# Regrouping a fused attention and adapter kernel: gate groups, DMA turns, squares, x copies and stores

## The chip, the cores and the metric

The kernel runs on one core of a Trainium2 chip. The metric is the device time of one execution in microseconds. A core has a matrix engine (PE, with weight loads shown as PEld), a vector engine (DVE), a scalar engine (ACT), a general engine (POOL) and a sync engine (SP). Each works through its own instructions in order. They wait for each other on semaphores. Transfers are issued from SP, ACT and POOL and run on 16 DMA engines.

## The reference

Two stages follow each other. The first is attention with a squared relu instead of a softmax; its result, with the heads side by side, is x. The second adds to each row of x the outputs of its two best of eight low-rank adapters.

```python
batch, n_heads, seq, head_dim = (8, 12, 448, 64)
scores = scale * np.matmul(q, k.transpose(0, 1, 3, 2))
attn = np.maximum(scores, 0.0) ** 2 / S
x = np.matmul(attn, v)                   # then (8 * 448, 768)
logits = x @ w_gate                      # 8 experts, the best 2 kept
w = softmax over the two kept logits
delta[rows of e] += w * ((x @ A[e]) @ B[e])   # A: 768 x 16, B: 16 x 768
return x + delta
```

## The kernel before, in words

**Tiling.** A batch has 448 rows. Its 12 heads are worked in three sets of four heads (a quad, q), two of them on each half of the 128 partitions. The 448 keys are cut into seven blocks of 64 (j). One step n is one batch, one quad and one key block. The last batch is cut once more, into its first 320 queries (one key block a step) and its last 128 (four key blocks a step). That makes 174 steps, numbered in the order in which they run: 21 for each batch, 27 for the last. n below 126 is batches 0 to 5, n from 126 batch 6, n from 147 batch 7.

**A step.** POOL issues the loads of q, k and v (L185). `tp` turns q and k on PE through the identity (L310), and DVE copies them out to qT (L324). `qk` makes the scores of four heads, keys on the partitions, in two PSUM banks (L449). `relu` scales them, applies the relu and writes bf16 into a tile of the pool `a`, on ACT (L468) or DVE (L470). `sq` squares a whole tile of `a` on DVE (L485). `pv` multiplies v with it and adds over the seven key blocks in PSUM (L516). After the last block `xt_copy` casts the result into `xt`, which holds x turned, channels on partitions (L544). The pairs of steps that share a tile of `a`, and so a square, follow the cycle 2, 2, 3 (`sqs`), at most 2688 columns (`GROUP`).

**The adapters.** The 3584 rows of x form 28 tiles of 128. A gate group of up to three tiles is worked at once. `z` multiplies x with the gate and all A (L560). On DVE come a top-8 per tile (`gmax`, L581) and the small operations `gd`, `gu`, `gt`, `gw` (L585 to L600); the sigmoid of ACT (`gsg`, L597) gives the two weights; `gzp` scales z (L604). `zt` turns it on PE (L622), and `zT` copies it out (L639). Then each tile is done in two halves of 384 columns. `b` (L705, L714) makes three matmuls with the identity that turn x back, and one product with B in float32 that shows as two MATMULs. `o` (L743) evacuates a half to a tile of the pool `osb` on ACT or DVE. `st` (L760) stores it.

**Turned tiles.** For tiles 15 to 23 (`xback`) the identity matmuls are left out. Instead SP turns x back with six DMA transposes for each three tiles (`xb`, L655), and the evacuation, then on DVE only, adds the turned x (L734). Each turn waits for the x copies of its tiles and, with `xlag=6`, for the store of the tile six before.

**The store.** Rows are permuted inside a batch: 64 consecutive rows of a tile are one j, and land in the output seven rows apart. So `st` issues two transfers of 64 rows for a tile. The last tile is stored as two halves, from SP and ACT. Tiles 24 and 26 are stored from ACT, all others from SP.

**Order.** `build` makes the operations with their dependencies and the pool buffers that they take and give. The string `ORDER` is a list written out ahead of time: every operation by name and number, with its PSUM bank (`@4`) and, where it can run on two engines, its engine (`:A`, `:D`). Each engine gets its operations in that order. Names such as `f64` are loads. A position in this list is told below by the relu it stands behind: "at relu140" means after relu140 and before relu141. `POOLS` gives the number of buffers: 11 for `a`, four for `osb`, three for `xb`.

Of the kernel before, what the change touches and what calls it, by code (L numbers as in the profile page):

```python
# [10 lines left out]
BF16 = mybir.dt.bfloat16  # L11
# [3 lines left out]
J = 7  # L15
CUT = 3
SPIN = 8
PH = 64
QUADS = 3
NB = 8  # L20
# [9 lines left out]
PARTS = {b: ((0, S, 1),) for b in range(NB)}  # L30
PARTS.update({7: ((0, 320, 1), (320, 448, 4))})


C = dict(late=6, xi=(), om=(), merge_x=0, sqs=(2, 2, 3), xback=(15, 23), xblat=1.4, xbdur=1.35, bx=8, xlag=6, xh=2, apart=3, apcap=1, gl=(3, 1), tqlat=2.0)
GROUP = 2688
POOLS = dict(qT=5, a=11, zp=2, zT=3, osb=4, w=3, q=5, k=5, v=8, xb=3)
# [3 lines left out]
f4 f3 f1 f0 f2 f6 f5 f8 f7 f11 f9 f10 f84@0 f12 f88 f85@2 f90 f89 f13 f87@4 qk0@6 f91 qk1@0 qk2@2 relu0:D qk3@4  # L40
f14 relu1:A relu2:D relu3:A tp2@6 f17 qk4@0 relu4:A te2 qk5@4 qk6@2 sq2 relu5:A tp3@6 f16 f86@0 relu6:A te3 sq0
qk7@0 f15 qk8@4 qk9@6 relu7:A tp4@2 relu8:D relu9:A f18 qk10@0 te4 qk11@4 relu10:A qk12@6 sq4 tp5@2 relu11:A f19
qk13@0 relu12:A te5 tp6@4 f26 relu13:A sq9 qk14@2 qk15@6 tp7 relu14:A f23 sq7 pv0@0 pv1 pv2 relu15:A pv3 qk16@2
te6 pv4 pv5 relu16:A f20 pv6 qk17@6 x13:D pv7@4 relu17:A qk18@2 sq11 pv8 f22 pv9 x12:A qk19@6 relu18:A pv10
qk20@0 relu19:D f21 pv11 relu20:A pv12 pv13 qk21@2 x27:A sq16 qk22@6 f27 qk23@0 relu21:A aw1@5 sq14 relu22:A f33
relu23:A x26:D qk24@2 tp8@6 ae1 f25 relu24:A qk25@0 sq18 qk26@4 tp9 relu25:A f55 pv14@2 pv15 pv16 relu26:A pv17
te8 qk27@0 pv18 f31 pv19 relu27:A pv20 sq23 qk28@4 qk29@6 x41:A f28 qk30@0 relu28:A x40:D aw0@3 sq25 relu29:A
f29 relu30:A qk31@4 tp10@6 ae0 tp11 relu31:A f32 sq21 qk32@0 qk33@2 relu32:A te10 pv21@4 pv22 f30 relu33:A pv23
qk34@0 sq30 qk35@6 relu34:A qk36@2 f37 relu35:D relu36:A qk37@0 pv24 pv25 pv26 relu37:A sq32 qk38@2 f35 tp12@6
pv27 relu38:A tp13 qk39@0 x55:A te12 f43 qk40@2 x54:A z0@5 relu39:A sq35 qk41@6 f34 z1 relu40:A qk42@0 relu41:D  # L50
z2 relu42:A qk43@2 f38 gmax0 relu43:A tp14@6 sq28 qk44@0 tp15 relu44:A f42 qk45@2 gd0 gu0 te14 relu45:A qk46@0
gt0 relu46:A f50 sq39 qk47@6 pv28@2 pv29 pv30 gsg0 pv31 relu47:A qk48@0 f24 pv32 pv33 gw0 sq44 pv34 relu48:A f48
qk49@6 x69:A gzp0 tp18@0 relu49:A tp19 sq37 f36 pv35@4 zt0@3 zt1 zt2 x68:A qk50@6 te18 zT0:A pv36 f41 pv37
relu50:A qk51@2 pv38 sq46 pv39 relu51:A pv40 qk52@0 f47 qk53@6 pv41 relu52:A tp16@2 x82:D tp17 relu53:A te16
qk54@0 b2@4 relu54:A sq49 f44 qk55@6 o2:A qk56@2 qk57@0 relu55:A relu56:D b0@4 f49 x83:A relu57:D qk58@6 o0:A
qk59@2 relu58:A z3@5 z4 f39 sq51 relu59:A qk60@0 qk61@6 z5 sq56 relu60:A b4@4 f40 relu61:A gmax3 qk62@2 sq58
b1@0 relu62:A f46 gu3 gd3 o4:A qk63@6 gt3 sq42 qk64@2 gsg3 o1:A b3@1 f65 relu63:A gw3 b5@4 gzp3 relu64:A sq60
f51 zt3@0 zt4 zt5 o3:A pv42@6 pv43 o5:A qk65@2 st2 pv44 zT3:A pv45 sq53 qk66@4 relu65:A pv46 pv47 pv48 tp20@0
relu66:A st4 qk67@2 tp21 x96:D x97:A f53 te20 pv49@4 relu67:A pv50 qk68@6 st0 pv51 pv52 relu68:A pv53 sq63 f66
pv54 pv55 qk69@0 qk70@2 x110:A relu69:D qk71@6 f45 relu70:A b6@4 relu71:A x111:D qk72@0 o6:D tp22@2 relu72:A  # L60
sq65 qk73@6 tp23 pv56@4 pv57 relu73:A f74 qk74@0 te22 pv58 pv59 relu74:A pv60 qk75@6 f79 pv61 sq67 pv62 relu75:A
qk76@2 b8@0 relu76:A x124:D qk77@6 f64 x125:A sq70 tp24@2 relu77:A tp25 qk78@4 z6@1 te24 f59 relu78:A qk79@6 z7
relu79:A o8:D qk80@4 qk81@2 f52 sq72 z8 relu80:A b10@0 relu81:A gmax6 sq77 f54 qk82@6 tp26@4 o10:A tp27 qk83@2
relu82:A gd6 gu6 b7@0 te26 f56 relu83:A qk84@6 gt6 o7:D qk85@4 gsg6 relu84:A qk86@2 gw6 f70 sq74 b9@0 relu85:A
pv63@6 pv64 relu86:A gzp6 pv65 qk87@4 pv66 sq79 pv67 relu87:A pv68 pv69 zt6@1 zt7 x139:A x138:D zt8 qk88@2 o9:A
qk89@4 zT6:D qk90@6 relu88:A st8 relu89:D tp28@0 tp29 relu90:A qk91@2 f80 te28 pv70@4 pv71 relu91:A pv72 pv73
qk92@6 f60 sq84 pv74 pv75 relu92:A pv76 qk93@0 b14@2 x153:D x152:A f58 relu93:A sq81 qk94@6 tp30@4 o14:A tp31
pv77@0 relu94:A pv78 f77 qk95@2 te30 pv79 pv80 relu95:A pv81 qk96@6 pv82 f57 sq91 pv83 relu96:A qk97@4 b11@2
relu97:D x166:A f67 b12@3 x167:A o11:A sq93 qk98@6 o12:A st10 qk99@0 qk100@4 relu98:A relu99:D b13@2 relu100:A
z9@3 st6 sq88 qk101@6 o13:A tp32@0 qk102@4 relu101:A tp33 b15@2 st12 f62 sq86 relu102:A qk103@6 o15:A te32 f61  # L70
qk104@4 relu103:A z10 z11 sq100 relu104:A qk105@0 f69 pv84@6 pv85 pv86 relu105:A gmax9 qk106@4 pv87 sq95 f72
pv88 relu106:A pv89 pv90 qk107@0 x181:A qk108@4 f63 gd9 gu9 x180:A relu107:D b16@2 relu108:A gt9 qk109@6 o16:D
f81 pv91@0 gsg9 pv92 relu109:A gw9 pv93 sq105 qk110@4 pv94 pv95 relu110:A pv96 f78 qk111@6 gzp9 pv97 relu111:A
x195:D zt9@2 zt10 qk112@4 sq98 x194:A zt11 f75 b17@3 relu112:A zT9:D qk113@6 o17:A sq102 pv98@0 qk114@4
relu113:A pv99 st16 tp36@2 pv100 tp37 relu114:A pv101 qk115@6 te36 pv102 pv103 relu115:A st14 pv104 tp34@4 tp35
f83 sq109 qk116@2 x209:A qk117@6 x208:A b20@1 relu116:A f68 te34 b22@0 relu117:A f71 sq114 o20:A qk118@2 qk119@4
qk120@6 relu118:A b21@1 f73 sq112 o22:A b23@2 relu119:A o21:D z12@3 sq107 relu120:A st20 qk121@0 qk122@4
relu121:A z13 relu122:D z14 o23:A qk123@6 pv105@0 gmax12 pv106 relu123:A qk124@4 gd12 pv107 gu12 pv108 gt12
sq116 pv109 relu124:A pv110 pv111 qk125@6 f82 b18@2 gsg12 relu125:A gw12 x223:D x222:A qk126@4 f76 o18:D qk127@6
relu126:A b19@1 gzp12 sq121 relu127:A zt12@0 zt13 zt14 qk128@2 pv112@4 pv113 o19:D relu128:A qk129@6 pv114  # L80
zT12:D pv115 st18 pv116 relu129:A pv117 sq123 pv118 tp38@2 qk130@0 x236:A tp39 qk131@6 st22 relu130:A b24@4 te38
relu131:A tp42@0 sq119 tp43 x237:A qk132@2 b25@6 relu132:A te42 xb90 b28@7 o24:A o25:A sq128 xb93 qk133@2 o28:A
qk134@4 tp40@0 relu133:A sq126 pv119@6 tp41 pv120 relu134:A pv121 xb91 qk135@2 te40 pv122 pv123 relu135:A pv124
pv125 qk136@4 x251:D xb94 qk137@0 x250:A b29@2 sq130 relu136:A b26@3 st24 relu137:A sq135 o29:A qk138@6 qk139@4
o26:A qk140@0 xb92 z15@2 relu138:A relu139:D z16 z17 relu140:A qk141@6 st28 gmax15 pv126@4 pv127 relu141:A gd15
pv128 gu15 qk142@0 gt15 sq133 pv129 pv130 gsg15 pv131 relu142:A xb108 qk143@6 pv132 gw15 b27@3 gzp15 x264:A
x265:D relu143:A zt15@2 xb111 zt16 zt17 sq137 pv133@0 o27:A qk144@4 tp44@6 zT15:A pv134 tp45 relu144:A xb95
qk145@2 pv135 te44 pv136 relu145:A pv137 qk146@4 pv138 pv139 st26 sq140 relu146:A z18@6 b30@7 x279:A sq142 z19
x278:A xb109 qk147@2 qk148@4 qk149@0 o30 relu147:A z20 sq144 b32@7 relu148:A xb112 relu149:A b33@2 gmax18 xb110
qk150@4 o32 qk151@0 relu150:A b31@3 gu18 o33 relu151:A gd18 qk152@4 sq149 st32 b34@7 relu152:A gt18 o31 gsg18  # L90
qk153@0 qk154@4 gw18 o34 relu153:A b35@2 st30 gzp18 relu154:A qk155@0 o35 pv140@6 relu155:A pv141 sq151 qk156@4
xb113 pv142 pv143 relu156:A qk157@2 qk158@0 pv144 pv145 relu157:D relu158:A pv146 tp46@4 tp47 x293:A x292:D
qk159@0 qk160@2 relu159:A zt18@7 te46 zt19 xb126 zt20 z21@6 relu160:A z22 sq156 zT18:A qk161@0 qk162@4 qk163@2
relu161:A xb129 b40@7 sq147 relu162:A z23 sq158 relu163:A qk164@0 xb127 pv147@4 pv148 pv149 relu164:A pv150
qk165@2 o40 pv151 pv152 relu165:A pv153 sq154 qk166@0 xb130 b41@7 relu166:A gmax21 x307:A gu21 qk167@2 gd21
pv154@0 sq163 x306:A pv155 pv156 st34 relu167:A pv157 pv158 qk168@4 gt21 o41 pv159 gsg21 pv160 b36@2 gw21 x320:A
gzp21 xb128 x321:A b38@3 sq161 relu168:A zt21@7 zt22 sq165 zt23 qk169@0 st40 zT21:A pv161@4 pv162 pv163
relu169:A pv164 qk170@6 o38 pv165 pv166 relu170:A o36 pv167 xb131 b37@3 x335:D x334:A sq168 qk171@0 qk172@6
relu171:A qk173@4 z24@2 o37 z25 relu172:A sq170 st36 b46@3 relu173:A b47@0 o46 b39@1 sq172 b44@3 o47 z26 o39
# [831 lines left out]
```

## Time and profile before

| | us |
|---|---|
| median of 3 runs (181.49 to 182.18) | 182.09 |
| the profiled execution | 182.88 |
| its span, first to last instruction | 180.8 |
| mean granted PE clock | 0.988 |

One row of the profile's group list is one kind of instruction: how often it ran, its busy time, the mean duration of one. These touch the change:

| group | count | busy us | mean ns |
|---|---|---|---|
| DVE square, 128 x 1792 (L485) | 45 | 48.2 | 1082 |
| DVE square, 128 x 2688 (L485) | 21 | 32.9 | 1572 |
| ACT relu, 128 x 896 (L468) | 132 | 114.6 | 990 |
| ACT cast of x, 128 x 448 (L544) | 28 | 16.1 | 616 |
| DVE cast of x, 128 x 448 (L544) | 14 | 8.7 | 618 |
| PE product with B, 128 x 384 (L714) | 112 | 47.5 | 515 |
| PE identity matmuls of x (L705) | 114 | 12.7 | 220 |
| ACT output copy, 128 x 384 (L743) | 26 | 13.1 | 523 |
| DVE output copy, 128 x 384 (L743) | 12 | 6.7 | 555 |
| DVE output add with turned x (L734) | 18 | 9.7 | 550 |
| SP issue of a turn (L655), median | 18 | | 1264 |
| SP issue of a store (L760), median | 52 | | 588 |

Instructions of one engine overlap: the next one starts before the last has ended, so the time from start to start, which the timeline gives, is less than a duration. A median turn lands 3.1 us after its issue starts.

### The profile page before, as it was taken

The numbers are of one execution on the slowest core, as the hardware profiler recorded it, in microseconds if no ns is written. First come the engines' busy times: TensorE is split into PE (matmuls) and PEld (weight loads), VectorE is DVE, ScalarE is ACT, GpSimd is POOL, SyncE is SP. The second block draws the span as 40 slices with busy tenths as digits, with TensorE's granted clock in tenths as the row PEclk, the third lists the DMA queues.
The fourth block names the chain that finished last, engine by engine and source line by source line (L and its number), as shares of the span: only waits on it lengthen the run. The fifth ranks groups of instructions, "written<-read, shape, count | busy, mean of one in ns | idle before, by whom it ended". The sixth has DMA issues, their size and how long they took to land.

```text
span 180.8 us, 7744 instructions
## 1 busy us (share of the span) xinstructions
PE 165.2 (91%) x3366; PEld 99.2 (55%) x3366; DVE 163.6 (90%) x254; ACT 156.4 (87%) x240; POOL 89.9 (50%) x155
## 2 busy tenths in 40 slices
PE   7777889788999999999999899999999999999990
PEld 2434466454555565655646475655666557676640
DVE  0799799999989999999999899999999999999740
ACT  3499899999999999999999999999999899992120
POOL 7998998979669377760877487340000000000000
PEclk9997899999999999999999999999999999999999
DMA  5999999999999999996599999997376579467875
GB/s 94 127 175 180 156 142 179 182 184 164 214 142 146 186 237 194 176 178 141 68 143 287 224 181 259 224 170 202 68 126 144 131 175 110 101 149 176 227 215 172
DMA packets 34450, 30.50 MB, mean 169 GB/s; under 512 B 11952, under 2 KB 30896, under 8 KB 34416
## 3 DMA queue, kind: packets, MB, share of 16 engines
q0 software_dynamic: 22000, 17.03, 64.9%
q1 hardware_dynamic: 11792, 11.90, 26.5%
q10 hardware_dynamic: 624, 1.08, 2.2%
q8 instruction: 26, 0.43, 1.0%
q14 instruction: 8, 0.07, 0.1%
HBM read 33.84 MB, written 11.01 MB: 248 GB/s over the span
## 4 chain that ended last, share of the span: by engine, by line
PE 51%; ACT 27%; POOL 7%; DMA 6%; issue 4%; DVE 3%; ACTq 0%; DVEq 0%; POOLq 0%
ACT a L468 24%; PE ps L714 18%; PE ps L449 11%; PE ps L516 10%; DMA q<-in_q_dram 6%; PE ps L560 4%; PE ps L310 3%; PE ps L705 3%; POOL q L185 3%; POOL k L185 3%; PE ps L622 2%; ACT osb L743 2%; DVE a L485 2%; ACT xt L544 1%; POOL k_rest L216 1%
## 5 line engine op out<-in xcount | busy, mean ns | idle before, releaser
L468 ACT ACTIVATE a<-ps 128x896 bf16<-128x896 f32 (+3 forms) x158 | 132.6, 952 | 3.7 <-PE ps L449 3.1
L485 DVE TENSOR_TENSOR a<-a 128x1792 bf16<-128x1792 bf16 (+3 forms) x75 | 89.0, 1200 | 0.0
L449 PE MATMUL ps<-qT 64*64 64x448 bf16 (+2 forms) x756 | 58.1, 342 | 3.9 <-ACT a L468 2.4
L714 PE MATMUL ps<-B,zT 128*128 128x384 f32 x112 | 47.5, 515 | 0.0
L516 PE MATMUL ps<-a,v 64*64 64x448 bf16 (+2 forms) x756 | 45.3, 335 | 1.6 <-DVE a L485 1.3
L449 PEld LDWEIGHTS <-qT 64*64 64x64 bf16 x756 | 25.1, 105 | 31.8 <-issue 23.2
L185 POOL DMA_DIRECT2D k<-in_k_dram x46 | 27.9, 629 | 18.2 <-PE ps L310 7.3
L185 POOL DMA_DIRECT2D v<-in_v_dram x48 | 29.0, 629 | 6.2 <-PE ps L449 1.8
L185 POOL DMA_DIRECT2D q<-in_q_dram x48 | 29.4, 651 | 4.9 <-DMA v<-in_v_dram 2.7
L516 PEld LDWEIGHTS <-v 64*64 64x64 bf16 x756 | 22.7, 108 | 9.0 <-issue 4.1
L324 DVE COPY qT<-ps 128x1792 bf16<-128x1792 bf16 x21 | 22.8, 1085 | 0.2
L544 ACT CAST xt<-ps 128x448 bf16<-128x448 f32 (+2 forms) x37 | 19.0, 554 | 2.9 <-PE ps L516 2.7
L743 ACT COPY osb<-ps 128x384 f32<-128x384 f32 x26 | 13.1, 523 | 7.1 <-PE ps L714 4.1
L714 PEld LDWEIGHTS ps<-B,zT 128*128 128x128 f32 x112 | 17.3, 190 | 3.3 <-issue 0.3
L470 DVE TENSOR_SCALAR a<-ps 128x896 bf16<-128x896 f32 (+1 forms) x16 | 16.9, 1067 | 0.5 <-PE ps L449 0.5
L310 PEld LDWEIGHTS <-q 64*64 64x64 bf16 x672 | 10.4, 111 | 6.3 <-issue 2.5
L560 PEld LDWEIGHTS <-xt 128*128 128x128 bf16 x168 | 10.5, 98 | 5.8 <-issue 4.7
L560 PE MATMUL ps<-awg,xt 128*128 128x136 bf16 x168 | 13.5, 223 | 0.0
L705 PEld LDWEIGHTS <-xt 128*128 128x128 bf16 x114 | 8.0, 98 | 9.9 <-issue 8.1
L310 PE MATMUL ps<-identb,q 64*64 64x64 bf16 x672 | 10.8, 196 | 2.5 <-DMA q<-in_q_dram 1.3
L705 PE MATMUL ps<-identb,xt 128*128 128x128 bf16 x114 | 12.7, 220 | 0.2
L544 DVE CAST xt<-ps 128x448 bf16<-128x448 f32 (+2 forms) x17 | 9.6, 571 | 2.2 <-PE ps L516 2.2
(47 smaller groups left out, 97.5 us busy)
## 6 DMA issues: line engine op xcount, KB each, us to landing
out_dram<-osb SPq DMA_DIRECT2D x50, 192.0 KB, 3.9
q<-in_q_dram POOLq DMA_DIRECT2D x48, 112.0 KB, 4.8
v<-in_v_dram POOLq DMA_DIRECT2D x48, 112.0 KB, 5.0
k<-in_k_dram POOLq DMA_DIRECT2D x46, 112.0 KB, 5.1
out_dram<-osb ACTq DMA_DIRECT2D x4, 192.0 KB, 2.9
B<-in_moe_B_dram POOLq DMA_DIRECT2D x1, 384.0 KB, 8.0
xb<-xt SPq DMA_TRANSPOSE x18, 3.1
a_raw<-in_moe_A_dram POOLq DMA_DIRECT2D x1, 192.0 KB, 5.2
```

The costliest lines, as they stand in the source:

```text
L185: nc.gpsimd.dma_start(out=t[g * PH : g * PH + PH], in_=k.qkv[w][b, g, :, 2 * q : 2 * q + 2, :])
L310: nc.tensor.transpose(k.ps_b[sl * PH : sl * PH + PH, o.banks[g], (w * J + j) * PH : (w * J + j) * PH + PH], source(w, j)[r, sl], k.identb[ ...
L324: nc.vector.tensor_copy(t.rearrange("p g w x -> p g (w x)"), k.ps_b[:, m.banks[0] : m.banks[0] + 2, : 2 * S])
L449: nc.tensor.matmul(out=bank(o, sl)[g * PH : g * PH + PH, at : at + w], lhsT=t[r, g, 1, j * PH : j * PH + PH], rhs=t[r, g, 0, x0:x1], start ...
L468: nc.scalar.activation(out, flat(qk_ops[n], w), ACTF.Relu, scale=k.relu_scale)
L470: nc.vector.tensor_scalar(out, flat(qk_ops[n], w), k.relu_scale, 0.0, op0=ALU.mult, op1=ALU.max)
L485: nc.vector.tensor_mul(a, a, a)
L516: nc.tensor.matmul(out=bank(head, g)[sl * PH : sl * PH + PH, :w], lhsT=vn[r, sl, j * PH : j * PH + PH], rhs=T["a", g0][r, x + sl * width(n ...
L544: evac(w, lambda cp, g=g: cp(k.xt[:, g * QUADS + q, b * S + x0 : b * S + x1], bank(src, g)[:, :w]), deps=[pv_ops[n]], free=[(src, g)], key ...
L560: nc.tensor.matmul(out=bank(zops[0])[:, t * ZW : t * ZW + ZW], lhsT=k.xt[:, do, 128 * tiles[t] : 128 * tiles[t] + 128], rhs=k.awg[:, do, : ...
L705: nc.tensor.matmul(out=out(h)[:, x * 128 : x * 128 + 128], lhsT=k.xt[:, 3 * h + x, c0 : c0 + 128], rhs=k.identb, start=(x == 0), stop=Fals ...
L714: nc.tensor.matmul(out=o, lhsT=T["zT", g0][:, zi], rhs=rhs, start=xb is not None, stop=True, skip_group_check=True,)
```

## The change

- **Gate groups** are no longer always three tiles. They have 3, 3, 3, 3, 2, 3, 2, 2, 3, 3 and 1 tiles (`gf`), so that a group ends where a batch ends. There are 11 instead of 10.
- **Turns.** Tiles 17 to 20 are turned four at once, then tiles 21 to 23 and 24 to 26 three at once (`tg`). Tiles 15 and 16 are no longer turned. There are 18 turns as before. The dependency on the store six tiles before goes. `xb` has two larger buffers instead of three.
- **Squares.** Steps 14 to 139 share a tile of `a` by 4 and 3 instead of 2, 2 and 3 (`sqp`, `GROUP` 3584). 75 squares become 57. `a` has eight larger buffers instead of eleven.
- **x copied whole.** For steps below 126 (`merge_x`) one cast of 128 x 2 x 448 from two banks takes the place of two casts of 128 x 448.
- **Stores.** A tile inside one batch is stored by one transfer of 2 x 64 rows. Only the four tiles that straddle two batches keep two transfers.
- **Order.** `ORDER` is written anew throughout, with the engine of the two-engine operations and the banks. The time estimates beside the operations serve only to make such a list. The loads' order on POOL changes; among others the memsets of `sel` come earlier. Several new switches (`fl`, `om2`, `idle`) are empty or unused.

The diff, cut to its core:

```diff
-PARTS = {b: ((0, S, 1),) for b in range(NB)}
-PARTS.update({7: ((0, 320, 1), (320, 448, 4))})
+PARTS = {b: ((0, S, 1, range(QUADS)),) for b in range(NB)}
+PARTS.update({7: ((0, 320, 1, (0, 1, 2)), (320, 448, 4, (0, 1, 2)))})
...
-C = dict(late=6, xi=(), om=(), merge_x=0, sqs=(2, 2, 3), xback=(15, 23), xblat=1.4, xbdur=1.35, bx=8, xlag=6, xh=2, apart=3, apcap=1, gl=(3, 1), tqlat=2.0)
-GROUP = 2688
-POOLS = dict(qT=5, a=11, zp=2, zT=3, osb=4, w=3, q=5, k=5, v=8, xb=3)
+C = dict(late=6, xi=(), om=(), merge_x=126, sqp=((14, (2, 2, 3)), (140, (4, 3)), (999, (2, 2, 3))), om2=(), fl=(), gf=(3, 3, 3, 3, 2, 3, 2, 2, 3, 3, 1), ai=4, tg=((17, 4), (21, 3), (24, 3)), sp=(), xbdur=1.45, bx=8, xh=2, apart=3, apcap=1, gl=(3, 1), tqlat=2.0)
+GROUP = 3584
+POOLS = dict(qT=5, a=8, zp=2, zT=3, osb=4, w=3, q=5, k=5, v=8, xb=2)
...
-    pair_of, n, turn = {}, 0, 0
+    pair_of, n, turn, sqs_ = {}, 0, 0, None
     while n < NS:
-        m = min(c["sqs"][turn % len(c["sqs"])], NS - n)
+        sqs = next(x for lim, x in c["sqp"] if n < lim)
+        if sqs is not sqs_:
+            sqs_, turn = sqs, 0
+        m = min(sqs[turn % len(sqs)], NS - n)
...
-                new("xb", ("xb", t0), [128, 3, DO, 128], BF16)
+                new("xb", ("xb", t0), [128, max(x for _, x in c["tg"]), DO, 128], BF16)
...
-                ts[do] = op(("SP",), c["xbdur"], lambda do=do: turn(do), kind="turn", deps=list(dict.fromkeys(deps)) + [st_of[t0 - c["xlag"]]],
+                ts[do] = op(("SP",), c["xbdur"], lambda do=do: turn(do), kind="turn", deps=list(dict.fromkeys(deps)),
...
+        (b0, j0), (b1, j1) = (divmod((c0 + r) // PH, J) for r in (0, PH))
+
         def st(e, c1=0, c2=2 * W):
-            r = 0
-            while r < 128:
-                b, x = divmod(c0 + r, S)
-                j, p = divmod(x, PH)
-                m = min(PH - p, 128 - r)
...
-                    out=k.out[b, j, p : p + m, c1:c2], in_=T["osb", tl][r : r + m, c1:c2])
-                r += m
+            dma = {"SP": nc.sync, "ACT": nc.scalar}[e].dma_start
+            if b0 == b1:
+                dma(out=k.out[b0, j0 : j0 + 2, :, c1:c2], in_=T["osb", tl][:, c1:c2])
+                return
+            for i, (b, j) in enumerate(((b0, j0), (b1, j1))):
+                dma(out=k.out[b, j, :, c1:c2], in_=T["osb", tl][i * PH : i * PH + PH, c1:c2])
...
-        m = min(c.get("gsz", 3), NT - t)
+        m = c["gf"][len(groups)] if len(groups) < len(c["gf"]) else min(c.get("gsz", 3), NT - t)
...
-            if c["xback"][0] <= g[0] <= c["xback"][1]:
-                turned(g)
+            for t0, m in c["tg"]:
+                if t0 == g[0]:
+                    turned(list(range(t0, t0 + m)))
             gate(g)
```

The end of `ORDER` before, and then after:

```
relu173:A b47@0 o46 b39@1 sq172 b44@3 o47 z26 o39
...
zT24:D st44 z27@6 o42 b52@7 o43 gmax27 b53@5 st42
gd27 gu27 o52:A gt27 gsg27 b50@4 gw27 gzp27 o53:D zt27@3 b51@2 st53 b48@5 o51:D b49@0 o50:A o48:D zT27:A st50
b54@1 o49:A st49 b55@7 o54:D st54 o55:D st55
```

```
relu173:A b42@2 o47 z24@3 sq172 z25 xb149 z26 pv168@4 o46 pv169 pv170@0
...
b49@0 o50 gw27 b51@5 gzp27 o49 zt27@1 b52@4 o51 st49 zT27:D b53@0 st50 o52 b54@5 o53 st53 b55@4 o54:D st54 o55:A
st55
```

## The prediction

> **What bounds the kernel now.** I read the page's busy line first, then the windows by stage, the timelines of the vector engine (DVE) and the scalar engine (ACT), the chain, and the DMA issues. The page:
>
> ```profile
> PE 165.2 (91%) x3366; PEld 99.2 (55%) x3366; DVE 163.6 (90%) x254; ACT 156.4 (87%) x240; POOL 89.9 (50%) x155
> ...
> ACT  3499899999999999999999999999999899992120
> ```
>
> Three engines near 90% look like one shared limit, but the slices say that ACT is full until the last four and then nearly idle. The windows at the times at which relu14, relu126 and relu173 run (found by counting ACT's relus: 11 lie before relu14, 112 before relu126) make three stretches:
>
> ```profile
> 16.00:119.00 103.00, 97.14 (x2091) 58.26 (x2092) 99.85 (x136) 101.14 (x149) 75.35 (x126) 0.98 1.10 182
> 119.00:162.00 43.00, 42.89 (x882) 27.02 (x881) 42.24 (x72) 41.31 (x69) 0.63 (x2) 1.00 0.68 138
> 162.00:176.00 14.00, 13.89 (x154) 8.64 (x152) 10.47 (x31) 3.66 (x12) 0.00 (x0) 1.00 0.74 197
> ```
>
> The columns are length, then PE, weight loads, DVE, ACT, POOL. In the first, ACT (101.1 of 103) and DVE (99.9) share the bound. In the second all three are at the limit, DVE with 0.8 us to spare. In the third only PE works without a gap, and the chain there is its output pieces: 0.17 us for three transposing matmuls, 0.70 for the product with B, 0.87 a half tile:
>
> ```profile
> 172.41 0.17 PE ps L705 x3
> 172.58 0.70 PE ps L714 x2
> 173.28 0.17 PE ps L705 x3
> 173.45 0.70 PE ps L714 x2
> ```
>
> Durations overlap, so I price work from start to start. ACT: two casts of x start 0.84 us ahead of what follows them, 0.42 each; seven relus of 896 then take 5.71, 0.82 each. DVE: a square of 2688 holds it from 36.82 to 38.29, 1.47 us, one of 1792 from 39.29 to 40.29, 1.00, so 896 columns cost 0.47 and a square's fixed part is 0.06:
>
> ```profile
> 38.27 1.14 ACT L544 CAST xt<-ps 128x448 bf16<-128x448 f32 x2
> 39.11 5.99 ACT L468 ACTIVATE a<-ps 128x896 bf16<-128x896 f32 x7
> 44.82 0.38 ACT L597 ACTIVATE sg<-t 128x24 f32<-128x24 f32 x1
> ```
> ```profile
> 36.82 1.54 DVE L485 TENSOR_TENSOR a<-a 128x2688 bf16<-128x2688 bf16 x1
> 38.29 1.08 DVE L324 COPY qT<-ps 128x1792 bf16<-128x1792 bf16 x1
> 39.29 1.08 DVE L485 TENSOR_TENSOR a<-a 128x1792 bf16<-128x1792 bf16 x1
> 40.29 1.08 DVE L470 TENSOR_SCALAR a<-ps 128x896 bf16<-128x896 f32 x1
> ```
>
> **The change, part by part.**
>
> *Squares of 4 and 3.* 75 become 57, over the same columns: 18 x 0.06 = 1.1 us less DVE. Before the first product of a group can start, its relus must all be done; with four that is up to 2 x 0.82 = 1.6 us later than with two. The list holds products 6 or more steps behind the relus, which covers it. Without that cover PE would wait up to 1.6 us a group. The a pool falls from 11 to 8 buffers; the tightest reuse is relu165, seven operations after the product that frees its buffer. ACT would wait there, with the relus queued behind.
>
> *x copied whole.* In batches 0 to 5, 24 casts on ACT become 12 and 12 on DVE become 6. No 896-column cast is in the trace; the nearest rows are the relus of that shape, 0.82 on ACT and 1.00 on DVE (a DVE cast of 448 starts 0.53 ahead of its successor). So ACT gains 24 x 0.42 - 12 x 0.82 = 0.2 us, DVE 12 x 0.53 - 6 x 1.00 = 0.4. Bounds by durations (616 and 990 ns) would be 2.9 on ACT; I keep the start-to-start value, as ACT is back to back. The Trainium skill speaks of this saving: "Perfetto Trace Analysis", Optimizing Scalar/DVE Operations, gives a per-instruction overhead of about 51 ns for the scalar engine on PSUM and 125 for DVE; by it the two would be 12 x 0.051 + 6 x 0.125 = 1.4 us instead of 0.6.
>
> *Eleven gate groups instead of ten.* One more d, u, t, w and product row on DVE: 0.07 + 0.09 + 0.09 + 0.10 and 0.06 fixed = 0.4 us; a sigmoid on ACT, 0.11. Tiles 12, 13, 15 and 16 no longer wait for the next batch. That readiness is hardly used: the output products of tiles 16 and 17 move from relu147 and relu151 to relu150 and relu157.
>
> *Who does what.* Evacuations of outputs: ACT 26 to 22 (0.36 each), DVE 30 to 34 (0.46 each); zT: ACT 6 to 8, DVE 4 to 3.
>
> *Stretch one, before relu126.* ACT: two relus more (+1.6), x (21 casts to 10 whole, -0.6), five outputs fewer (-1.8), two zT more (+0.7): -0.1. DVE: two relus fewer (-2.0), x (11 to 5, -0.8), five outputs more (+2.3), two zT fewer (-0.9), squares (14 fewer, two units more, +0.1): -1.3. ACT is the fuller one, so the work itself gives between 0 and 1.3; to that comes ACT's idle 0.9 us at 18.7, where the transposes waited for a load of batch 1: they now come four relus later. Bounds: 0 to -2.2. I take -0.9.
>
> *Stretch two.* DVE: two relus more (+2.0), a zT and the gate rows (+0.9), two outputs and three squares fewer (-1.1), x +0.1: +1.9. PE: two half tiles more (1.4), identities on 11 halves instead of 7 (tiles 15 and 16 lose their turn, 0.7), four products (0.8), less one z and two transposes (0.8): +2.1. With 0.8 us free on DVE this stretch grows by 1.1. Bounds 0 and +2.1.
>
> *Tail.* After relu173 PE now has 12 half tiles, 2 with identities, for 14 with 8: -2 x 0.70 - 6 x 0.17, and two z more (+0.7): -1.7. DVE gets one output more (13 adds and copies, 6.0 us, with gates and squares about 10 of 12): it stays under PE. Bounds -2.4 (the z find room) and -0.7 (DVE becomes the bound). The new turns of tiles 24 to 26 must land: the last one follows the last x copy by a turn, a store and itself, 1.26 + 0.59 + 3.1 (its median landing) = 5.0 us; ahead of the half that uses it PE has 7 half tiles, 1.4 us of z and 1.3 of products, 7.6. It is hidden by 2.6 us; a turn of four tiles, by size 3.1 x 4/3 = 4.1 us, has 20 relus.
>
> *Queues.* A store is issued once (588 ns) instead of twice, for 23 of the 27 whole tiles (four straddle batches) and for the last tile's two halves. SP is not on the chain, except at the end: the last store's second issue goes, -0.6, while its transfer doubles to 192 KB (2.9 against 2.7 us on ACT's queue). I take -0.3; bounds -0.6 and +2.5 (192 KB of a_raw landed in 5.2). The turns no longer wait for a store, but in SP's order stores stand behind turns that wait for x: tile 4's moves from relu88 to relu140, tile 9's from relu128 to relu164. Each keeps one of four output buffers so long. Behind them SP has the later turns and stores; who would wait is the evacuation of a later tile, on DVE or ACT with everything queued there. By the list a buffer is reused 4 relus or more after its store, until the tail.
>
> *Loads.* POOL's order is new and the memsets of sel come before k of batch 1. Six loads stand 5 or 6 relus (4 to 5 us) ahead of use, three before; landing is 4.8 to 5.1 us. Cost 0 to 0.5 us each; I take none, the queue of relus (three ahead) covers it.
>
> **Sum.** -0.9 + 1.1 - 1.7 - 0.3 = -1.8 us. The profiled execution took 182.88 us (span 180.8 and 2.1 around it), so 181.1 on its footing; it lies 0.8 above the median of 182.09, and on the median's footing the forecast is 180.3.
>
> **Rivals.**
>
> *B: work is only moved.* Totals hardly change: PE -0.4, ACT -0.9, DVE +0.3 us. If stretch one is held by ACT (-0.1 and the gap stays) and stretch two pays PE's 2.1, then 0 + 2.1 - 1.7 - 0.3: 182.2. For it: ACT's 101.1 of 103. Against: DVE's relief there and the gap.
>
> *C: single stores land too late (slower).* No row shows a store whose outer extent is two; all before have 64 rows. The rows:
>
> ```profile
> out_dram<-osb SPq DMA_DIRECT2D x50, 192.0 KB, 3.9
> ...
> B<-in_moe_B_dram POOLq DMA_DIRECT2D x1, 384.0 KB, 8.0
> ```
>
> 3.9 us for a half, 8.0 for the one transfer of 384 KB. The place is the tail, where four output buffers turn over: a tile holds one for 1.4 us of products, 0.55 of evacuation and the landing, so a tile every (1.95 + 3.9) / 4 = 1.46 us now, about PE's own 1.40. Above 3.9 the buffers decide: at 8.0 a tile takes 2.5, the last four tiles 4 x 1.1 = 4.4 more, and the last half by the 192 KB row 2.5 more: 187. Against: the larger landing was measured with the DMA engines full (share 1.0), and in the tail the halves land in 2.9. I forecast 3.9. A rule of the Trainium skill speaks for C and far beyond: "DMA: Bandwidth & Descriptors", Why a DMA increments its semaphore by 16 and not by 1, says a transfer uses the largest number of engines up to 16 that divides the slowest extents of both sides, here 2 and 128, so two engines. By it the 24 tiles would put 4.7 MB on each of two engines, at the stores' 15.5 GB/s an engine (11.90 MB in 26.5% of 16 x 180.8 us) 300 us of stores, and an end near 360 us; no run here shows such a transfer.
>
> *D: the new order stalls.* Loads 5 relus ahead, eight a buffers, squares of four: six waits of 0.5 us with ACT behind: +3, 183.3. For it: a load with eight relus' lead still held PE 0.34 us at 94.5. Against: all of PE's waits on loads sum to 2.0 us.
>
> **Numbers.** Forecast 0.50 (180.3, alone 178 to 181.2), B 0.18, C 0.20, D 0.12. 0.5% (0.9 us, about what a measurement can tell) puts the forecast under faster, B under same, C and D under slower: 0.50, 0.18, 0.32. The range reaches from 177.6 (the forecast's lower bounds, most of them at once) to 186.0 (D, and C up to a landing of 7 us); it leaves out C beyond that and a little below, 0.15 to 0.2.
>
> **What would show it.** Squares of 3584 near 2.0 us and 57 of them; whole casts that hold ACT 0.82; relu126 about 1 us earlier, relu173 no earlier, the tail from relu173 to the last half 12 us. Wrong if stores take over 5 us to land and evacuations wait for them, if PE waits for v, q or k loads, or if ACT idles for buffers of a.

## The result, and the profile after

The changed kernel takes **309.87 us** (median of 6, 306.83 to 311.15) against 182.09 (6, 181.49 to 182.99): ratio 1.6998, 95% interval 1.6912 to 1.7084. The forecast was 180.3, range 177.6 to 186.0. The profiled execution took 306.83 us, its span is 305.1. Medians here and below are of all executions, while ratios leave out those more than 1.5% above the fastest of the same kernel (two of four in `e11`).

The page after, first the busy line, then the slices of ACT, the granted clock and the DMA engines:

```profile
PE 191.3 (63%) x3360; PEld 108.8 (36%) x3360; DVE 165.0 (54%) x238; ACT 157.5 (52%) x227; POOL 89.9 (29%) x155
...
ACT  3899999999184596640348972436273000000000
...
PEclk9599999999778699885568997859599595575555
DMA  7999999948658978473119769911929391131110
```

DVE and ACT have almost the same work as before (163.6 and 156.4) in a span 124 us longer: they wait. PE is busy 26 us longer (165.2 before) with six matmuls fewer, at a mean granted clock of 0.794 for 0.988. The stretches of before, and one near the end (length, then PE, weight loads, DVE, ACT, POOL, clock, DMA share, GB/s):

```profile
16.00:119.00 103.00, 85.90 (x1813) 49.78 (x1813) 83.53 (x97) 87.69 (x118) 67.04 (x114) 0.93 0.95 147
119.00:162.00 43.00, 23.07 (x340) 12.04 (x340) 18.08 (x21) 16.50 (x24) 7.85 (x14) 0.69 0.45 83
162.00:176.00 14.00, 13.71 (x290) 8.55 (x290) 12.05 (x17) 12.96 (x21) 0.24 (x1) 0.99 1.08 99
284.00:300.00 16.00, 0.00 (x0) 0.00 (x0) 0.00 (x0) 0.00 (x0) 0.00 (x0) 0.50 0.13 51
```

The last line is the case in small. From 284 to 300 us no engine runs; only stores drain, with a share of 0.13 of 16 DMA engines, two engines, at 51 GB/s, 25.5 each. One store of 384 KB thus holds two engines for 7.7 us, and 24 of them 185 us. SP and ACT both store here: the queue of SP shows 6.9% of 16 engines' time, that of ACT 6.0%, together two engines and not two each. The waits (us in total, times, longest) and the row of the stores:

```profile
ACT osb L769 <- DMA out_dram<-osb: 44.9, 5, 32.2
...
DVE osb L769 <- DMA out_dram<-osb: 27.6, 5, 8.7
...
DVE osb L760 <- DMA out_dram<-osb: 20.3, 4, 7.0
```
```profile
out_dram<-osb SPq DMA_DIRECT2D x22, 384.0 KB
```

An evacuation waits up to 32 us for one of the four output buffers, 92.8 us in 14 waits, and everything behind it on its engine waits too. The small sizes of the forecast hold; a square of 3584 and a whole cast of x:

```profile
33.48 2.01 DVE L487 TENSOR_TENSOR a<-a 128x3584 bf16<-128x3584 bf16 x1
```
```profile
106.02 0.90 ACT L558 CAST xt<-ps 128x896 bf16<-128x896 f32 x1
106.81 1.75 ACT L470 ACTIVATE a<-ps 128x896 bf16<-128x896 f32 x2
```

The cast holds ACT 0.79 us from start to start (forecast 0.82).

### The profile page after: what moved, and what is told of

Read it like the earlier page. It is cut to its first block, busy times and chain, and to the rows that moved or that the text cites. A ratio compares the mean times of both kernels' runs of the same rounds, so it can differ in the third digit from the quotient of the medians.

```text
span 305.1 us, 7654 instructions
## 1 busy us (share of the span) xinstructions
PE 191.3 (63%) x3360; PEld 108.8 (36%) x3360; DVE 165.0 (54%) x238; ACT 157.5 (52%) x227; POOL 89.9 (29%) x155
## 4 chain that ended last, share of the span: by engine, by line
DMA 52%; PE 15%; ACT 12%; issue 7%; DVE 4%; POOL 3%; SPq 0%; DVEq 0%; ACTq 0%; POOLq 0%
DMA out_dram<-osb 36%; ACT a L470 10%; DMA xb<-xt 5%; DMA q<-in_q_dram 4%; PE ps L451 4%; PE ps L518 4%; DMA v<-in_v_dram 4%; DMA k<-in_k_dram 3%; PE ps L733 2%; PE ps L312 2%; ACT xt L558 1%; POOL q L184 1%; DVE a L487 1%; POOL k L184 1%; PE ps L578 1%
## 5 line engine op out<-in xcount | busy, mean ns | idle before, releaser
L470 ACT ACTIVATE a<-ps 128x896 bf16<-128x896 f32 (+2 forms) x158 | 132.6, 935 | 35.5 <-PE ps L451 34.5
L487 DVE TENSOR_TENSOR a<-a 128x2688 bf16<-128x2688 bf16 (+4 forms) x57 | 85.9, 1524 | 0.0
L451 PE MATMUL ps<-qT 64*64 64x448 bf16 (+2 forms) x756 | 65.2, 370 | 21.6 <-ACT osb L769 14.7
L733 PE MATMUL ps<-B,zT 128*128 128x384 f32 x112 | 57.7, 616 | 14.8 <-DVE osb L760 14.7
L518 PE MATMUL ps<-a,v 64*64 64x448 bf16 (+2 forms) x756 | 49.6, 360 | 10.8 <-issue 6.7
L760 DVE TENSOR_TENSOR osb<-ps,xb 128x384 f32<-128x384 f32 x20 | 10.6, 552 | 34.7 <-DMA out_dram<-osb 20.3
L769 DVE COPY osb<-ps 128x384 f32<-128x384 f32 x14 | 7.7, 553 | 30.5 <-DMA out_dram<-osb 27.6
L472 DVE TENSOR_SCALAR a<-ps 128x896 bf16<-128x896 f32 (+2 forms) x16 | 16.9, 1060 | 1.5 <-PE ps L451 1.3
L312 PE MATMUL ps<-identb,k 64*64 64x64 bf16 x644 | 11.9, 208 | 6.6 <-DMA k<-in_k_dram 5.3
L724 PEld LDWEIGHTS <-xt 128*128 128x128 bf16 x108 | 8.1, 107 | 17.2 <-issue 16.5
```

Of the source, the lines that this page charges most:

```text
L312: nc.tensor.transpose(k.ps_b[sl * PH : sl * PH + PH, o.banks[g], (w * J + j) * PH : (w * J + j) * PH + PH], source(w, j)[r, sl], k.identb[ ...
L451: nc.tensor.matmul(out=bank(o, sl)[g * PH : g * PH + PH, at : at + w], lhsT=t[r, g, 1, j * PH : j * PH + PH], rhs=t[r, g, 0, x0:x1], start ...
L470: nc.scalar.activation(out, flat(qk_ops[n], w), ACTF.Relu, scale=k.relu_scale)
L472: nc.vector.tensor_scalar(out, flat(qk_ops[n], w), k.relu_scale, 0.0, op0=ALU.mult, op1=ALU.max)
L487: nc.vector.tensor_mul(a, a, a)
L518: nc.tensor.matmul(out=bank(head, g)[sl * PH : sl * PH + PH, :w], lhsT=vn[r, sl, j * PH : j * PH + PH], rhs=T["a", g0][r, x + sl * width(n ...
```

## The experiments

Each stands beside runs of the kernel before on the same chip (medians 181.2 to 182.0).

### The stores: alone, and taken out

`e1`, the changed kernel without its single-transfer store:

```diff
-            if b0 == b1:
-                dma(out=k.out[b0, j0 : j0 + 2, :, c1:c2], in_=T["osb", tl][:, c1:c2])
-                return
```

> The changed kernel with every store as two transfers of 64 rows again; all else as changed. Theory (a single transfer with an outermost extent of 2 runs on 2 of 16 DMA engines, as the last 16 us of the changed kernel's profile show by a DMA share of 0.13 and 51 GB/s): the time falls back to the forecast's sum, 178 to 182 us. Rival D (the new order stalls by itself: late stores, loads close to their use, eight a buffers): 190 us or more even with halves. Rival E (the turns without their wait on a store hold up SP): SP still blocked for 8 to 10 us a time between 160 and 260 us.

**190.88 us**, ratio 1.0501 (1.0448 to 1.0553). The single transfers are 119 of the 128 us. But the rest of the change costs 9 us, where the forecast's sum without its term for the stores says 1.5 less.

`e2`, the kernel before with that branch added:

> The kernel before with one change: the 23 tiles inside one batch, and the two halves of the last one, are stored by one transfer of 2 x 64 rows. Theory: 9.4 MB go through two engines at 51 GB/s together, 185 us of transfers that begin at 62, so the end is no earlier than 247 us, and 270 to 320 with the buffers' waits. Rival D: 182 to 185 us, since the order is the old one.

**307.13 us** (one run). The stores do it alone.

### Why: how many engines a store gets

Three runs cut each 64-row store of the kernel before in two, `m = min(PH - p, 128 - r)` becoming 62 and 2, 48 and 16, or 57 and 7 rows; bytes and pattern of a row stay.

> The kernel before, each 64-row store cut into 62 and 2 rows; the address pattern stays that of before. Theory in its sharper form (the number of engines is the largest up to 16 that divides the outermost extent): 62 and 2 both give two engines, 11.0 MB at 51 GB/s are 216 us, the end no earlier than 278 us, 285 to 340. Rival F (the interleaved pattern of 2 x 64 rows is slow, not the count): as the 48 and 16 kernel, 182 to 190 us.

> The control: the kernel before, each 64-row store cut into 48 and 16 rows, so as many issues as with 62 and 2. Theory: both extents give 16 engines, so only SP's issues double (58 more at 0.59 us, off the path except 0.6 at the end): 182 to 185 us. Rival (more and smaller transfers cost by themselves): 195 us or more.

> The kernel before with every 64-row store cut into 57 and 7 rows. Theory (a transfer is spread over the largest number of engines up to 16 that divides its outer extent, here 3 for 57 rows and 7 for 7, and each engine moves 25.5 GB/s of a store): an estimate from the runs so far is the work of the busiest engines: loads 112 us (62% of 181 us, the same for all 16) and stores 56 x 57 x 3 KB on 3 engines at 76.5 GB/s, 128 us, together 240 us; the same sum gave 289 us for the single-transfer stores (span 305) and 328 us for 62 and 2 rows (span 336), so 248 to 256 us here. Rival 1 (only the number of issues counts, as with 48 and 16 rows): 192 to 200 us. Rival 2 (any row count that isn't a multiple of 16 is as slow as two engines): 310 us or more.

**338.48, 194.24 and 257.21 us** (one run each). The late stretch of 62 and 2, and of 57 and 7 (columns as above):

```profile
300.00:330.00 30.00, 0.00 (x0) 0.00 (x0) 1.58 (x3) 0.48 (x1) 0.00 (x0) 0.50 0.13 52
```
```profile
240.00:252.00 12.00, 0.00 (x0) 0.00 (x0) 0.00 (x0) 0.00 (x0) 0.00 (x0) 0.50 0.24 72
```

62 rows drain with two engines, 57 with three and a little; 72 GB/s is close to 3 x 25.5. The third time was foretold as 248 to 256 from the work of the busiest engines and came out at 257: the price follows the number of engines. Transfers of 64 or 48 rows, which 16 divides, do not have it.

The Trainium skill states the rule: "DMA: Bandwidth & Descriptors", Why a DMA increments its semaphore by 16 and not by 1: the largest number up to 16 that divides the slowest extents of both sides. The runs agree: two engines for an extent of 2 and for 62, three for 57. It adds that SP's and ACT's transfers always take the lowest-numbered ones; the drain, where both queues together show two engines, and the sum for 57 rows, which puts all on the same three and came within 1.2 us of its upper end, agree with that.

48 and 16 rows missed its 182 to 185 by 9 us, for a second reason:

```profile
170.07 19.95 SPq L761 DMA_DIRECT2D out_dram<-osb  x28
```

28 issues on SP take 20 us, 0.71 each. Four issues of a tile no longer fit under the 1.40 us that PE needs for it. In the kernel before two of them (1.18 us) just do. SP falls behind accordingly: its last store is issued 5.4 us after the last evacuation has ended, in the kernel before 0.5 us after.

### Where the other 9 us are: turns at the end, late loads

`e6`: `e1` without the turns of tiles 24 to 26. `e8`: `e1` with four pairs of loads exchanged. `e9`: both.

```diff
-tg=((17, 4), (21, 3), (24, 3))
+tg=((17, 4), (21, 3))
-xb144 ... xb147 ... xb145 ... xb148 ... xb146 ... xb149
-o48 ... o50 ... o49 ... o51 ... o52 ... o53
+o48:A ... o50:D ... o49:A ... o51:D ... o52:A ... o53:D
```
```diff
-f77 ... f73 ... f53 ... f74 ... f62 ... f61 ... f71 ... f68
+f53 ... f61 ... f77 ... f62 ... f74 ... f73 ... f68 ... f71
```

> The changed kernel with the old two-transfer stores, and tiles 24 to 26 no longer turned (their x is added on TensorE as before; ACT and DVE take their six evictions in turn). Theory (the 190.9 of the split-store kernel comes mostly from SP's queue at the end, six turns of 1.3 to 2.2 us each among two store issues a tile; without them SP has 1.2 us of issues a tile against 1.4 us of TensorE work): 5 to 8 us less, 183 to 186 us, and the tail after relu173 shorter by at least 4 us. Rival (the split-store kernel is late for its order and its loads in the middle, the queue at the end only follows): 189 to 192 us.

> The changed kernel with the old two-transfer stores; four pairs of loads change places, so that k4.2, q5.2, k5.2 and k6.1 are issued ahead of k7.1, q7.0, k7.0 and k6.2, which are used much later. Theory (two loads land late, about 88 and 107 us, and hold back the scores: 2 us; the rest is SP's queue at the end): 188.5 to 190 us, with no wait of TensorE for a k or q load over 0.5 us after 80 us. Rival 1 (the end is set by SP's queue alone, so that work arriving 2 us earlier is lost there): 190 to 192 us. Rival 2 (the loads are the larger part): 183 to 187 us.

> Both edits in one: tiles 24 to 26 not turned, and the four pairs of loads exchanged. Theory (queue at the end and late loads add up): 181 to 184 us, no more than 1.5 us above the kernel before. If one of the two hides the other: within 0.7 us of the better single edit. Rival (neither is the cause; the new groups and turns themselves are slower): 187 us or more.

**183.78** (ratio 1.0073, 1.0028 to 1.0118), **190.6** (1.0419, 1.0331 to 1.0506) and **182.18** (1.0029, 0.998 to 1.0078). The late turns cost 7 to 8 us. What the loads are worth can't be told from nothing: alone the medians differ by 0.3 us, with the turns gone by 1.6, and the intervals overlap both times. The late load in `e1`, on PE:

```profile
87.86 0.41 PE L312 MATMUL ps<-identb,k 64*64 64x64 bf16 x26 [1.71 <-DMA k<-in_k_dram]
```

Other executions with the loads in this order show the wait as 1.27 us (`e5`), 0.97 (`e14`) or not at all (`e6`, `e11`, `e13`). With the loads exchanged PE waits for none between 80 and 120 us in `e8`, and 0.35 us for one in `e9`.

### What the late turns hold up

SP's queue at the end of `e1` (start, length, then the issues; `e8` shows the same pattern about 2.5 us earlier):

```profile
163.80 7.40 SPq L673 DMA_TRANSPOSE xb<-xt  x4
171.25 2.50 SPq L783 DMA_DIRECT2D out_dram<-osb  x4
173.85 2.56 SPq L673 DMA_TRANSPOSE xb<-xt  x2
176.51 10.24 SPq L783 DMA_DIRECT2D out_dram<-osb  x10
```

Before the first of these six turns SP stands idle for 3.5 us, until DVE has added the last half of tile 20 (at 163.7), which gives back one of the two buffers of `xb`; the copies of x that this turn needs had ended at 161.2. `e5`, `e8`, `e11`, `e13`, `e14` and `e17` show the same gap. No run of these orders has a third buffer, as the kernel before has, so what this wait costs stays open.

My first reading was that turns and stores share one queue. `e5` gives the stores of tiles 21 to 23 to ACT (and sets them elsewhere in the order); `e11` puts those of tiles 18 and 19 behind the last turn.

```diff
-STORES = {24: 'ACT', 26: 'ACT'}
+STORES = {21: 'ACT', 22: 'ACT', 23: 'ACT', 24: 'ACT', 26: 'ACT'}
```
```diff
-st36 ... st38 ... xb146 ... xb149
+xb146 ... xb149 st36 st38
```

> The changed kernel with the old two-transfer stores, tiles 24 to 26 turned as in the change, and the stores of tiles 21, 22 and 23 issued by ACT in place of SP. Theory (what costs is that stores and turns share SP's queue): 3 to 6 us less than 190.9, 185 to 188 us, and SP's queue done with the turns by about 174 us. Rival 1 (it is the turns' own time from issue to landing that is late, whatever the queue): 190 to 192 us. Rival 2 (issues on ACT cost ACT as much as SP gains, since ACT evicts in the tail): 189 to 192 us with ACT the engine ahead of most waits there.

> The changed kernel with the old two-transfer stores (190.9 us); the stores of tiles 18 and 19 are put on SP's queue behind the last turn of tiles 24 to 26, and no longer ahead of the last two. Theory (the last turn stands behind four store issues of 0.6 us): the last turn is issued 2.4 us earlier, by 174.2 us of the span, 188 to 189.5 us. Rival (the output buffers of tiles 18 and 19, four in all, come free 2 to 3 us later instead and hold back the additions): 190 to 193 us.

**193.15** (1.059, 1.053 to 1.0651) and **192.56** (1.0487, 1.042 to 1.0555). Both miss. In `e11` the last turn is out by 171.0, 5 us earlier, and DVE waits all the same:

```profile
174.50 1.02 DVE L760 TENSOR_TENSOR osb<-ps,xb 128x384 f32<-128x384 f32 x2 [5.61 <-DMA out_dram<-osb]
```

So it is not the last turn alone. Both edits left the four first turns, 7.4 us in `e1`, ahead of the stores of tiles 18 and 19. In `e5` the turns themselves also took longer to issue (min/median/max ns), `e1` first, then `e5`:

```profile
L673 SPq DMA_TRANSPOSE xb<-xt x6: 1186/1296/2166, 163.8 to 175.2; - x6
```
```profile
L673 SPq DMA_TRANSPOSE xb<-xt x6: 1178/1710/3234, 161.7 to 176.8; - x6
```

The longest, 3.23 us, had stores issued by ACT beside it. But `e5` has one of 2.47 us and `e1` one of 2.17 with none beside them, and in `e13` and `e17` a turn beside ACT's issues took 1.31 and 1.29. What lengthens them is not shown.

`e13` moves exactly the stores of tiles 18 and 19 to ACT (`STORES` with 18 and 19, and `st37` after `o39`, `st39` after `relu170`). `e14` leaves them and takes six buffers (`osb=4` to `osb=6`). `e16` is `e9` with six buffers.

> The changed kernel with the old two-transfer stores (190.9 us); the stores of tiles 18 and 19 alone go to ACT's queue, so that they no longer stand behind the first four turns of tiles 24 to 26. Theory (those four turns hold SP for 7 us, and two of the four output buffers wait for the stores behind them): the two stores are issued 3 to 5 us earlier, and the time is 186 to 188.5 us. Rival (the turns themselves end too late for tiles 24 to 26, whatever the stores do): 190 to 192 us, with the wait moved from the stores to the turned x.

> The changed kernel with the old two-transfer stores (190.9 us), and six output buffers in place of four; order and queues as they were. Theory (stores that stand behind the turns cost time only because four buffers wait for them): the waits of DVE and ACT for a store in the tail, 14.7 us together, go, and the time is 183 to 187 us. Rival (SP's queue has more to issue in the tail than fits, so that the last store is late whatever the buffers): 189 to 191.5 us, the last store issued at 186 us as before.

> The split-store kernel with loads exchanged and no turns of tiles 24 to 26 (182.2 us), and six output buffers in place of four. Theory (without late turns TensorE ends the tail and no store is waited for): 181.5 to 182.5 us, no change. Rival (buffers still hold back an eviction in the middle): 180.5 to 181.5 us.

**186.9** (1.0301, 1.0254 to 1.0347), **189.03** (1.0435, 1.0385 to 1.0485), **181.9** (1.0032, 1.0003 to 1.0061). The two stores behind the first turns are 4 us. The buffers alone are 1 to 2 us, not clear of noise, where their theory said 4 to 8; without late turns they make no difference. With six buffers in `e14` the addition no longer waits for a store, but for a late turn, nearly as long:

```profile
174.21 1.02 DVE L760 TENSOR_TENSOR osb<-ps,xb 128x384 f32<-128x384 f32 x2 [4.10 <-DMA xb<-xt]
```

The late turn and the late stores hide each other. `e13` mends both: its last turn is out by 169.4, and no addition waits for turned x there.

`e17` puts all together: `e13`, six buffers and the loads exchanged.

> The changed kernel with the old two-transfer stores and the late turns of tiles 24 to 26 kept; the stores of tiles 18 and 19 on ACT's queue (186.9 us by itself), six output buffers (189.0 by itself) and the four pairs of loads exchanged. Theory (late turns cost time only through the stores behind them and the late loads): 181.5 to 184 us. Rival (the turns' own end, after the last copies of x, holds tiles 24 to 26): 185 to 187 us with the additions waiting for turned x.

**184.71 us** (1.0155, 1.0112 to 1.0198), above its theory's 184, below its rival's 185, and 2.8 us above the kernel before. The end of its chain, in order of time:

```profile
173.79 0.71 PE ps L733 x2
174.50 0.02 issue
174.53 0.57 DVE osb L769
175.09 0.24 ACTq L783
175.34 0.04 issue
175.38 1.48 ACTq L783
...
176.96 0.48 ACT osb L769
```

PE's last product, not on this chain, ends at 175.35, 0.5 us earlier than in the kernel before (175.89):

```profile
174.49 0.86 PE L733 MATMUL ps<-B,zT 128*128 128x384 f32 x2
```

But the last evacuation is on ACT, behind the two store issues of tile 26, and starts 1.6 us after that end (before: on DVE, at 175.92, at once). A second place lies further up: relu173 starts at 163.55 for 162.45 in `e9`, and the chain stands at 159.42 to 160.73 on ACT's issues of the stores of tiles 18 and 19. Both are read from the trace. No run put that evacuation or those issues elsewhere, so what each is of the 2.8 us is not shown.

### Parts alone

`e12` is the kernel before with whole x copies (`merge_x=126`, each where the first of its two halves stood); `e18` puts them where the second stood. At that place some copies come after their banks have gone to later scores, so that part of x is other data; it is read for its time alone. `e15` is `e9` with two half copies again (`merge_x=0`, `x12:A` to `x12:A x13:D` and so on). `e10` is `e9` with tiles 14 to 16 turned, early, where SP is idle (`tg=((14, 3), (17, 4), (21, 3))`, `o28` to `o33` on DVE, relu139, 142 and 156 on ACT, the turns of tiles 21 to 23 after `o33`).

> The kernel before with one part of the change alone: the x of the first 126 score units is copied with one instruction of 896 columns in place of two of 448 (18 fewer instructions in the order kept as it was). Theory of the prediction's sum (18 copies of 0.82 to 1.00 us in place of two of 0.49 to 0.55 us: 0.2 us of ACT and 0.4 us of DVE, of which part is on the path): 0 to 0.6 us less, 181.4 to 182 us. Rival (two banks of PSUM are held until the one copy ends, so that the next scores wait): 182.5 us or more.

> The kernel before with whole x copies for the first 126 units, as in the run of 189.1 us, but each copy at the place in the order where the later of its two halves stood, and not the earlier. Theory (the copy came too early on its engine, ahead of relus that the products wait for): 182 to 185 us. Rival (it is not the place but the length of one copy, which holds two banks and one engine for 0.9 us in an order written for two engines side by side): 187 to 191 us.

> The split-store kernel with loads exchanged and no turns of tiles 24 to 26 (182.2 us), and x of the first 126 score units copied in two halves again, one on ACT and one on DVE, at the place where the whole copy was. Theory of the prediction's sum (a whole copy is worth what the fixed parts of a second copy cost): 182.2 to 182.9 us. Rival 1 (two halves on two engines at once free the banks 0.4 us sooner and are better): 181 to 182 us. Rival 2 (every such edit to an order that was written for something else costs several us, as whole copies did in the order of before): 185 to 190 us.

> The split-store kernel with loads exchanged and without turns of tiles 24 to 26 (182.2 us), and tiles 14 to 16 turned in their place, between relu118 and relu126, where SP has little to do; their six additions of x on TensorE go, three copies of scores move from DVE to ACT, five evictions from ACT to DVE, and the turns of tiles 21 to 23 come after tile 16's last addition. Theory (a turn is worth what it takes off TensorE, 6 x 0.17 = 1.0 us, where SP is idle and TensorE is busy all the time): 180.8 to 181.6 us. Rival (DVE becomes what ends last there, or the turns of tiles 21 to 23 come too late): 182 to 184 us.

**189.07** (1.0397, 1.034 to 1.0453), **190.44** (1.0487, 1.042 to 1.0554), **190.88** (1.0517, 1.0482 to 1.0553) and **188.73** (1.0357, 1.0302 to 1.0411). All four miss their theory, by 5 to 8 us, in the same direction; `e12` and `e18` land in the range of their rivals. Whole copies cost 7 us in an order written for halves, halves cost 9 in one written for whole copies; a later place does not mend it (`e18`). ACT's wait for scores, in the kernel before, then in `e12`:

```profile
ACT a L468 <- PE ps L449: 3.1, 7, 0.9
```
```profile
ACT a L468 <- PE ps L449: 8.5, 14, 1.8
```

And in `e9`, then in `e15`:

```profile
ACT a L470 <- PE ps L451: 3.7, 9, 1.3
```
```profile
ACT a L470 <- PE ps L451: 8.5, 19, 1.1
```

The work is nearly the same (ACT is busy 157.0 us in `e12` for 156.4, 157.0 in `e15` for 156.9); the waits are new. `e12` loses its time before relu126 (126.0 for 118.5), `e10` between relu150 and relu173 (142.2 and 168.9 for 140.7 and 162.4 in `e9`). Through what step of the order each wait comes I have not settled, and so the worth of one part cannot be read from a run that changes it alone.

## Why the prediction was wrong, point by point

- **Queues: "I forecast 3.9."** This step failed, and with it the forecast. The term for the stores was -0.3, bounds -0.6 and +2.5, and measured +119 us (`e1`). The landings behind it, of 64-row stores and of a load of 128 rows, are of transfers whose outer extent 16 divides; they could not bound a store on two engines, which holds them 7.7 us at 25.5 GB/s each. Rival C was right in kind (0.20), its 187 wrong by the same error. The prediction named the skill's rule and left it out of its range. The skill's rule was right; my estimate of 360 us by it was too high, because the 15.5 GB/s an engine is not a rate of the stores alone: the row (11.90 MB, 26.5%) is SP's whole queue, with the 18 turns in it. From 172 to 180 us before, where only stores are under way, the same working gives 17.7 (1.65 MB in 72.9% of 16 x 8 us), and the drain 25.5.
- **Tail: "It is hidden by 2.6 us."** Failed as well. The last turn was set 1.26 + 0.59 us behind the last copy of x; in `e1` the last copy that it needs starts at 165.87, and its issue starts at 175.21, 9.3 us later, with four turns and four store issues of its queue between, and the first of those turns had waited for a buffer of `xb`. That late turn itself held an addition only 0.9 us in `e1`. Worse is what the sum had left out: the stores behind the first four turns. Together 7 to 8 us (`e6`, `e8` and `e9`); about 4 of them are two stores (`e13`).
- **"SP is not on the chain, except at the end."** True, and underrated: there its issues set the time (`s48`, `e13`).
- **Loads: "I take none."** k of batch 4 stood 6 relus ahead and held PE 1.71 us in `e1`, 1.27 and 0.97 in two other runs, not at all in three; its cost is not told from nothing.
- **Stretch one, -0.9.** Right. In `e9` relu126 starts at 116.75, before at 118.53: -1.8, inside 0 to -2.2, and in eight other runs, which differ from it in stores, loads, late turns or output buffers alone, -0.5 to -2.0. Only `e1`, with the late load, has it later (120.6).
- **Stretch two, +1.1.** Mis-sized. relu173 starts at 162.45 in `e9` and 162.15 before, so the stretch grew by 2.1: PE's whole +2.1, the upper bound. The step set DVE's 0.8 us to spare against the growth, though PE, by its own row, had none (42.89 of 43 us busy; 43.00 in `e9`).
- **Tail of PE, -1.7.** Right: from relu173 to the end of the last product 13.7 us before, 11.8 in `e17`. It did not reach the end, as relu173 came later and the last evacuation was then held.
- **Whole copies and squares.** Their durations were right (0.79, 2.01 us). What they are worth in the order is open (`e12`, `e15`).
- **Rivals B and D.** With stores split, late turns out and loads exchanged the time is 182.18. That this is B's 182.2 is luck: B's sum kept the tail's -1.7 with the late turns hidden, and the stores' -0.3, and `e9` has neither the late turns nor the single stores. D expected stalls for loads, buffers of `a` and squares, +3 us; of these the runs show the late load alone, and `e1` no wait for `a`. Of the 9 us left in `e1`, 7 to 8 go with the late turns.

No version was faster than the kernel before: the nearest, `e9` and `e16`, stand at 1.0029 and 1.0032.

## What to carry to other kernels

Before two transfers are merged to save an issue, look at the outer extent of both sides: an extent of 2 gives two DMA engines, and a share of 0.13 in a stretch where nothing else runs is how the profile says so. A price for a form of transfer that the trace does not hold is not bounded by forms that are cut otherwise; where a stated rule says a factor of eight, it belongs in the range. In a tail where SP's issues just fit, ask of every instruction put on its queue which stores stand behind it and who waits for their buffers. And in an order written ahead of time an edit of one part alone cost 6 to 9 us here, in the old order and in the new one: such a run does not tell what the part is worth as long as the order around it is not written anew.

## What the runs showed of the hardware

- PE's granted clock was 0.50 in the drain, where PE had nothing to do, and 0.69 from 119 to 162 us, where it was busy 23 of 43 us. 3360 matmuls took 191.3 us of PE, 3366 before 165.2. How much of the 128 us this is no run tells.
- A turn's issue on SP took 1.18 to 2.17 us in `e1`, with no store issued by ACT beside it, and up to 3.23 in `e5`, beside ACT's stores; but 1.31 and 1.29 beside them in `e13` and `e17`. What sets it is not shown.
- By packet time, stores moved 25.5 GB/s an engine on two engines (the drain) and 17.7 on sixteen (before, 172 to 180 us); SP's whole queue before, turns included, gives 15.5. Why an engine moves less there is not shown.
- Stores from SP and from ACT that get two engines each were on two engines together: 6.9% and 6.0% of 16 engines' time in the drain.
